# Identity matmuls ahead of the decay products, three more raw buffers, a later range check and an earlier copy of the ends in a GateLoop and ReLU-squared kernel

## The chip, the cores, the metric

One core of one Trainium2 chip. The metric is device time in microseconds (us) of one execution. "Kernel before" and "changed kernel" are the two sides.

## The reference

A gated linear recurrence with a complex decay per head channel, then a feed-forward block with squared ReLU:

```python
# q, k, v, a_re, a_im: (4, 8, 768, 48); w_in (384, 2048), w_out (2048, 384)
mag = np.sqrt(a_re * a_re + a_im * a_im)
scale = np.minimum(mag, 0.999) / (mag + 1e-06)
a_re_n, a_im_n = (a_re * scale, a_im * scale)
for t in range(S):
    new_re = ar * S_re - ai * S_im
    new_im = ar * S_im + ai * S_re
    S_re, S_im = (new_re + kv, new_im)          # kv = outer product of k[t], v[t]
    y[:, :, t] = np.einsum('bhd,bhde->bhe', q[:, :, t], S_re)
# ... y becomes x of (3072, 384)
h = x @ w_in
r = np.maximum(h, 0.0)
out = (r * r) @ w_out
```

## The kernel before

The work is cut into eight units of 384 tokens (n = 0 to 7). Each unit has a decay chain on VectorE (DVE) and ScalarE (ACT), four pairs of heads (h numbers the two heads of a pair) on TensorE (PE), and the dense products `h` (x by w_in) and `o` (g by w_out).

The kernel does not leave the order of instructions to the compiler. Every piece of work is a *step* with an engine, an assumed cost, a rank and a list of dependencies; a list scheduler written in the kernel walks them and fixes each engine's order:

```python
def step(key, engine, cost, rank, deps, fn, lag=None, bank=None, until=None):
    steps[key] = (engine, cost, ..., rank, deps, fn, bank, until)
# lay_out(): picks, per engine, the ready step that can start first; rank decides among near ties
for _, key in lay_out():
    emit(steps[key][5])          # fn() issues the instructions, in this order
```

`deps` decide only *where in its engine's order* a step is put. At run time an instruction waits for the data and buffers that it touches, and for nothing else.

The decay chain of a unit first sums logs inside groups of tokens (`in..`), copies the groups' ends to `last` (`e1`), transposes them on PE (`tot`), copies those to `e` on ACT, forms scan products on DVE (`product`, ten stages, writing `e`), and transposes back on PE (`bk`). After that PE adds the halves of complex products (`P`):

```python
one("iq", "ACT", act_cost(2 * NEL), lambda z: [(f"in{W - 1}3",)],      # squares
    lambda z: act.activation(out=whole(u["fa", z]), in_=whole(u["a", z]), func=AF.Square))
one("e1", "ACT", act_cost(2 * HH * D),                                 # copy of the ends
    lambda z: [(f"in{W - 1}3",), ("ap", n - 1, 0), ("ap", n - 1, 1)],
    lambda z: ends(z, 0))
...
product([NM, G - 1, 3], rest_of, rest_of, ...)                         # the last of ten stages
...
add(("bk", n, j), "PE", 330, deps, lambda j=j: transpose(...), rank=-3000, bank="tr", ...)
```

The weights arrive as 64-bit floats, 384 KB a piece, 16 pieces of w_in and 16 of w_out, and DVE and ACT convert them between the other work of units 0 and 1. A piece of w_out (i >= NF) is fetched into one of a few raw buffers once a conversion has freed it:

```python
else:
    deps = [("cv", i - (NF - NF // 2 if i < NF + NRAW else NRAW), 2)]
step(("fetch", i), "SP" if i >= NF else "POOL", ...)
```

In the last unit all 32 pieces are fetched again to check their range (`look`), into buffers of the chain, which is over by then:

```python
step(("look", i), "POOL", 800, 10 ** 6, [("inspect", i - 4), ("ap", n, 0), ("ap", n, 1)],
     lambda i=i: look(i), 5500)
```

Each pair of heads ends in `ypair` (PE), a copy to `yt` (ACT) and a transfer of its rows into `xT`, which `h` reads.

## Time and profile before

| | before |
|---|---|
| median of its runs | 766.58 us (4 runs, 765.14 to 768.22) |
| span of the profiled run | 765.2 us |
| PE busy | 702.8 us |
| PE waits of unit 0, up to 49 us | some 45 us |
| PE waits for unit 1's chain, 147 to 152 us | 5.08 us |
| PE wait in the last unit, before 605.81 us | 2.26 us |

The lines behind the table are shown in the prediction. PE is the bound nearly everywhere, so what counts is where it idles and where its clock is halved. The clock is read best from the distance of like instructions: a pair of `P` instructions starts every 0.49 us at full clock and every 0.96 us at half.

### The profile page before, as it was taken

To read this page: it belongs to the slowest core of one execution; us is meant where nothing else is said; L and a number is where in the kernel's file an instruction comes from. 1 tells how busy PE (TensorE), PEld (TensorE's weight loads), DVE (VectorE), ACT (ScalarE), POOL (GpSimd) and SP (SyncE) were. 2 spreads that over 40 slices of the span, in tenths; PEclk is the share of its full clock that TensorE was granted. 3 is DMA by queue.
4 is the path that set the end of the run, shared out by engine and by line. 5 is a ranking of instruction groups with operands and counts; after the bars stand their busy time and mean duration, and the time that the engine had idled before them with its cause. 6 is when DMAs were issued, how large, how long until landed. Compare 5 with 4: busy or idle time off the path is not lost.

```text
span 765.2 us, 9943 instructions
## 1 busy us (share of the span) xinstructions
PE 702.8 (92%) x3538; PEld 471.7 (62%) x3538; DVE 506.9 (66%) x1200; ACT 407.9 (53%) x754; POOL 114.3 (15%) x165
## 2 busy tenths in 40 slices
PE   0259999799999999999999999999999899999996
PEld 0138555477567766866776686568668555555553
DVE  4889988986688889579776966988992654000000
ACT  6646494346946676851877187746665103402500
POOL 5003100043004014010310121040011431000000
PEclk9999999989999999999999999999999999999999
DMA  9507760045007114220710252062023684000000
GB/s 271 182 18 227 236 220 12 22 145 145 1 1 255 38 50 159 84 57 21 249 47 17 92 178 53 0 204 82 27 74 112 212 292 136 3 18 14 0 11 24
DMA packets 39196, 76.25 MB, mean 100 GB/s; under 512 B 10881, under 2 KB 25313, under 8 KB 39137
## 3 DMA queue, kind: packets, MB, share of 16 engines
q0 software_dynamic: 14336, 53.88, 22.4%
q1 hardware_dynamic: 24672, 21.49, 9.2%
q8 instruction: 30, 0.49, 0.3%
q14 instruction: 30, 0.24, 0.1%
q10 hardware_dynamic: 128, 0.15, 0.1%
HBM read 56.62 MB, written 14.16 MB: 93 GB/s over the span
## 4 chain that ended last, share of the span: by engine, by line
PE 82%; DVE 10%; ACT 2%; DMA 2%; issue 1%; ACTq 0%; DVEq 0%; SPq 0%
PE h L1344 31%; PE o L1361 28%; PE sa L1238 6%; PE tq L1225 5%; PE kv L1252 3%; PE ypair L1274 3%; PE ypair L1279 2%; PE P L1111 2%; DMA xT<-yt 2%; DVE fa L991 2%; DVE e L998 1%; DVE fa L843 1%; PE bk L937 1%; PE tot L937 1%; DVE fb L816 1%
## 5 line engine op out<-in xcount | busy, mean ns | idle before, releaser
L1344 PE MATMUL h<-xT,w 128*128 128x384 f32 x768 | 255.5, 487 | 1.9 <-DMA xT<-yt 1.9
L1361 PE MATMUL o<-w,g 128*128 128x384 f32 x768 | 255.3, 488 | 0.0
L1361 PEld LDWEIGHTS o<-w,g 128*128 128x128 f32 x768 | 143.8, 191 | 94.5 <-issue 1.5
L1344 PEld LDWEIGHTS h<-xT,w 128*128 128x128 f32 x768 | 142.8, 190 | 95.0 <-issue 3.6
L1351 ACT ACTIVATE g<-h 128x384 f32<-128x384 f32 x128 | 62.2, 486 | 86.2 <-PE h L1344 86.0
L1230 ACT COPY QKT<-tq 96x512 f32<-96x512 f32 x96 | 76.6, 871 | 44.7 <-PE tq L1225 43.8
L1366 ACT COPY ot<-o 128x384 f32<-128x384 f32 x24 | 11.5, 477 | 124.4 <-PE o L1361 122.9
L1354 ACT ACTIVATE g<-g 128x384 f32<-128x384 f32 x128 | 66.1, 523 | 2.9
L1244 DVE TENSOR_TENSOR A<-sa,mask 128x384 f32<-128x384 f32 x64 | 35.3, 553 | 39.7 <-PE sa L1238 38.4
L991 DVE TENSOR_TENSOR fa<-e 128x192 f32<-128x192 f32 (+4 forms) x144 | 47.8, 371 | 18.4 <-ACT e L964 16.2
L1238 PE MATMUL sa<-QKT 96*128 96x128 f32 x384 | 54.7, 283 | 0.6 <-DVE QK L1117 0.6
L1238 PEld LDWEIGHTS sa<-QKT 96*128 96x128 f32 x384 | 48.1, 191 | 7.7 <-issue 2.4
L1225 PE MATMUL tq<-ident,QK 128*96 128x128 f32 x384 | 51.2, 273 | 0.9 <-ACT QKT L1230 0.9
L1225 PEld LDWEIGHTS tq<-ident,QK 128*96 128x96 f32 x384 | 42.6, 127 | 9.8 <-issue 5.6
L937 PE MATMUL tot<-ident,last 128*128 128x128 f32 x72 | 12.2, 295 | 31.4 <-ACT last L862 27.1
L1274 PE MATMUL ypair<-A,v 128*48 128x128 f32 x384 | 37.7, 281 | 3.3 <-ACT yt L1284 2.3
L808 DVE TENSOR_TENSOR fb<-fa 128x576 f32<-128x576 f32 x32 | 24.0, 753 | 22.2 <-ACT fa L904 12.2
L816 DVE SCALAR_TENSOR_TENSOR fb<-fb 128x576 f32<-128x576 f32 x48 | 35.0, 752 | 5.5 <-ACT fb L811 5.2
L1128 POOL DMA_DIRECT2D rows<-QK x20 | 12.7, 636 | 171.2 <-DVE QK L1117 171.2
L998 DVE TENSOR_TENSOR e<-fa,fa 128x96 f32<-128x96 f32 (+6 forms) x160 | 35.6, 284 | 2.6
L811 ACT ACTIVATE fa<-fb 128x576 f32<-128x576 f32 x48 | 31.2, 675 | 8.7 <-DVE fb L808 7.3
L1117 DVE TENSOR_TENSOR QK<-qk,fa 128x576 f32<-128x576 f32 x48 | 33.1, 751 | 0.0
(105 smaller groups left out, 828.8 us busy)
## 6 DMA issues: line engine op xcount, KB each, us to landing
rows<-QK POOLq DMA_DIRECT2D x12, 576.0 KB, 3.8
raw<-in_moe_w_in_dram POOLq DMA_DIRECT2D x16, 384.0 KB, 8.0
raw<-in_moe_w_out_dram SPq DMA_DIRECT2D x16, 384.0 KB, 4.0
look<-in_moe_w_in_dram POOLq DMA_DIRECT2D x16, 384.0 KB, 5.4
look<-in_moe_w_out_dram POOLq DMA_DIRECT2D x16, 384.0 KB, 4.3
out_dram<-ot SPq DMA_DIRECT2D x24, 192.0 KB, 1.9
v<-in_v_dram POOLq DMA_DIRECT2D x18, 192.0 KB, 4.2
a<-in_a_re_dram POOLq DMA_DIRECT2D x12, 288.0 KB, 3.5
```

Of the source, the lines that this page charges most:

```text
L816: dve.scalar_tensor_tensor(out=f[dst[-1]], in0=f[2] if i == 0 else f[dst[0]], scalar=scalar, in1=f[by], op0=ALU.add if i else ALU.mult, op ...
L991: dve.tensor_tensor(out=t, in0=x(e), in1=y(e)[:, j].unsqueeze(1) .to_broadcast(shape), op=ALU.mult)
L998: dve.tensor_tensor(out=dst(u["e"])[:, r], in0=temp(0)[:, r], in1=temp(1)[:, 1 - r], op=ALU.add if r else ALU.subtract)
L1225: nc.tensor.transpose(ps[:, 2 * j + h], src, ident)
L1230: act.copy(out=u["T", i].rearrange("r z (p c) -> r c z p", c=W)[:, c], in_=u["tq", i, c])
L1238: nc.tensor.matmul(sa[:, j], lhsT=T[:, 2 + h, ts(j, C)], rhs=T[:, h, ts(j, C)], start=True, stop=True)
L1244: dve.tensor_tensor(out=u["A", i][:, h], in0=u["sa", i, h], in1=mask3, op=ALU.mult)
L1274: nc.tensor.matmul(ypair[64 * h:64 * h + D, ts(j, C)], lhsT=u["v"][:, j, 2 * i + h], rhs=A[:, h, j], start=True, stop=S_j is None)
L1344: nc.tensor.matmul(u["h", f], lhsT=w1[:, f, m], rhs=u["xT"][:, m], start=(m == 0), stop=(m == NM - 1))
L1351: act.activation(out=t, in_=u["h", f], func=AF.Relu)
L1354: act.activation(out=u["g", f], in_=u["g", f], func=AF.Square)
L1361: nc.tensor.matmul(u["o", c], lhsT=u["g", f][:, ts(c, C)], rhs=w2[:, f], start=(f == 0), stop=(f == NF - 1))
```

## The change

Intent: keep PE's clock up by dummy matmuls before `bk` and `P` of units 0 and 1; feed the conversions of w_out from eight raw buffers instead of five; let the decay chain go on sooner by copying the ends before the squares; keep the range check's fetches from the last rows of xT. The core of the diff (cuts marked):

```diff
+    LENT = {NF + NRAW: "A", NF + NRAW + 1: "A", NF + NRAW + 2: "xT"}
 def fetch(i):
+        if i in LENT:                        # raw buffer borrowed from A tiles or an xT tile
+            ... = pool_.tile(shape, F32, name=tag, tag=tag)
 def weight_steps():
+            elif i in LENT:
+                deps = [("mix", 0, NP - 1), ("xT", 0, NP - 1, 1)]
+            elif i < NF + NRAW:
+                deps = [("cv", i - (NF - NF // 2), 2)]
             else:
-                deps = [("cv", i - (NF - NF // 2 if i < NF + NRAW else NRAW), 2)]
+                deps = [("cv", i - NRAW - (len(LENT) if i < NF + 2 * NRAW + len(LENT) else 0),
+                         2)]
 ...
             step(("look", i), "POOL", 800, 10 ** 6, [("inspect", i - 4), ("ap", n, 0),
-                 ("ap", n, 1)], lambda i=i: look(i), 5500)
+                 ("ap", n, 1)] + [("xT", n, NP - 1, h) for h in range(2)], lambda i=i: look(i),
+                 5500)
 ...
-        one("iq", ...)
-        one("e1", ...)
+        one("e1", ...)
+        one("iq", ...)
 ...
+        if n < 2:
+            def busy():
+                ps = dp.tile([C, L], F32, name="busy", tag="d")
+                for j in range(NM):
+                    nc.tensor.matmul(ps[:, ts(j, C)], lhsT=ident, rhs=ident, start=True,
+                                     stop=True)
+            for j in range(BUSY):            # BUSY = 9
+                add(("busy", n, j), "PE", 640,
+                    [("scan", n, 4, "plus", 1), ("busy", n, j - 1)], busy, rank=10 ** 6,
+                    bank="d", until=("busy", n, j))
 ... (the A step of unit 1's first pair and the xT steps of unit 2 get ("cv", f, 2) as deps)
```

More of the change, by code (lines that the diff above doesn't have):

```diff
@@ L653, in fetch @@
             return
-        raws[i] = (wst.tile([C, DM, 2], U32, name="raw", tag="raw")
-                   if i >= NF or NF // 2 <= i < FIRST else
-                   gp.tile([C, DM, 2], U32, name="raw", tag="g"))
+        if i in LENT:
+            pool_, tag, shape = {"A": (pr, "A", [C, 2, NM, C]),
+                                 "xT": (xp, "xT", [C, NM, L])}[LENT[i]]
+            t = pool_.tile(shape, F32, name=tag, tag=tag)
+            raws[i] = (t.rearrange("p a b c -> p (a b c)") if tag == "A" else
+                       t.rearrange("p a b -> p (a b)"))[:, 0:2 * DM].bitcast(U32).rearrange(
+                           "p (n two) -> p n two", two=2)
+        elif i >= NF or NF // 2 <= i < FIRST:
+            raws[i] = wst.tile([C, DM, 2], U32, name="raw", tag="raw")
+        else:
+            raws[i] = gp.tile([C, DM, 2], U32, name="raw", tag="g")
         queue.dma_start(
@@ L902, in chain_steps @@
             lambda z: measure(2 + z, parts(z)[3]))
+        one("e1", "ACT", act_cost(2 * HH * D),
+            lambda z: [(f"in{W - 1}3",), ("ap", n - 1, 0), ("ap", n - 1, 1)],
+            lambda z: ends(z, 0))
         one("iq", "ACT", act_cost(2 * NEL), lambda z: [(f"in{W - 1}3",)],
@@ L905, in chain_steps @@
                                      func=AF.Square))
-        one("e1", "ACT", act_cost(2 * HH * D),
-            lambda z: [(f"in{W - 1}3",), ("ap", n - 1, 0), ("ap", n - 1, 1)],
-            lambda z: ends(z, 0))
         one("ia", "DVE", D1, lambda z: [("iq",)], add_squares)
@@ L1319, in pair_steps @@
                  bank="sc", until=("A", n, i, h))
-            step(("A", n, i, h), "DVE", 480, -20, [("sa", n, i, h)],
+            step(("A", n, i, h), "DVE", 480, -20, [("sa", n, i, h)] + (
+                [("cv", f, 2) for f in LENT if LENT[f] == "A"] if x == NP else []),
                  lambda h=h: scored(h))
@@ L1333, in pair_steps @@
             step(("xT", n, i, h), "ACT" if aside(h) else "SP", 600 * len(list(pieces(h))), -24,
-                 [("y", n, i), ("h", n - 2, NF - 1)], lambda h=h: place(h), lag=2400)
+                 [("y", n, i), ("h", n - 2, NF - 1)]
+                 + [("cv", f, 2) for f in LENT if LENT[f] == "xT" and n == 2],
+                 lambda h=h: place(h), lag=2400)
     def dense_steps(u):
@@ L1433, in fast_path @@
     CONV = (500, 700)
+    BUSY = 9
     for b in range(B):
```

## The prediction

> **What bounds the kernel now.** I read the page first, then the waits of PE, then the timelines around each of its large waits, and last the windows of the stretch in which the second weights are converted.
>
> ```profile
> PE 702.8 (92%) x3538; PEld 471.7 (62%) x3538; DVE 506.9 (66%) x1200; ACT 407.9 (53%) x754; POOL 114.3 (15%) x165
> PE 82%; DVE 10%; ACT 2%; DMA 2%; issue 1%; ACTq 0%; DVEq 0%; SPq 0%
> ```
>
> PE is busy for 702.8 of 765.2 us. Only 62.4 us of idle time, and time lost to a half clock, can be won without touching the dense products. PE's waits say where the idle time is:
>
> ```profile
> PE tot L937 <- ACT last L862: 27.1, 1, 27.1
> PE bk L937 <- DVE e L998: 15.9, 2, 10.8
> PE tot L937 <- ACT last L864: 4.1, 2, 3.9
> PE ypair L1274 <- ACT yt L1284: 2.3, 1, 2.3
> ```
>
> Some 45 us lie ahead of 49 us, before the first unit's decay chain on DVE (scan of products, `e`) gives PE anything. The second wait of `bk` is 15.9 - 10.8 = 5.1 us at 147 to 152 us, where PE has used up unit 0's dense work and unit 1's chain is not done. The 2.3 us are in the last unit. Between 192 and 600 us PE has 407.06 of 408 us busy: nothing to win there. So I look at three places: unit 0 up to 86 us, unit 1 at 147 to 161 us, unit 7 at 603 to 612 us. PE has work queued behind each of them, so a microsecond won there is a microsecond of the end.
>
> The timeline of PE at unit 1 shows the clock besides the gap (start, duration, engine, instruction, count, idle time before it):
>
> ```profile
> 152.12 1.41 PE L937 MATMUL bk<-ident,e 128*128 128x128 f32 x6 [5.08 <-DVE e L998]
> 154.18 1.33 PE L1111 MATMUL P<-fa,ident 128*128 128x288 f32 x2 [0.65 <-DVE fa L1098]
> 155.30 1.17 PE L1111 MATMUL P<-fb,minus 128*128 128x288 f32 x2
> ...
> 160.94 0.65 PE L1111 MATMUL P<-fa,ident 128*128 128x288 f32 x2
> 161.43 0.65 PE L1111 MATMUL P<-fb,ident 128*128 128x288 f32 x2
> ```
>
> From start to start a pair of P instructions takes 0.96 us at first and 0.49 us from 159.1 us on: half clock, then full. Unit 0 looks the same: 0.96 us a pair from 49.19 us, 0.49 us from 53.2 us.
>
> The end of the kernel has the third place, first in the timeline of ACT, then in that of PE:
>
> ```profile
> 605.27 0.48 ACT L1284 COPY yt<-ypair 112x384 f32<-112x384 f32 x1 [5.81 <-DMA xT<-yt]
> 605.81 0.43 PE L1274 MATMUL ypair<-A,v 128*48 128x128 f32 x4 [2.26 <-ACT yt L1284]
> 606.28 0.64 PE L1274 MATMUL ypair<-A,v 128*48 128x128 f32 x4
> ```
>
> The xT rows that must leave a `yt` buffer were issued at 599.01 us and landed 6.19 us later in the chain of waits, while their median is 2.2 us. In that stretch POOL issues `look` fetches of the range check, 384 KB each. PE waits 2.26 us for it, and then goes on at half clock (four `ypair` take 0.43 us from start to start in place of 0.22).
>
> The windows around the conversion of the second weights (PE, PEld, DVE, ACT, POOL busy; clock, DMA share, GB/s):
>
> ```profile
> 86.00:100.00 14.00, 13.24 (x41) 7.90 (x42) 13.61 (x32) 11.11 (x24) 0.00 (x0) 1.00 0.96 324
> 100.00:113.00 13.00, 13.00 (x42) 7.64 (x41) 9.90 (x23) 12.06 (x26) 0.00 (x0) 1.00 0.66 207
> 113.00:124.00 11.00, 11.00 (x36) 6.50 (x35) 10.31 (x19) 5.57 (x13) 0.00 (x0) 1.00 0.14 43
> ```
>
> DVE is nearly full except for 3.1 us at 100 to 113 us and 0.7 us at 113 to 124 us. The unit 1 chain shares DVE with the conversions, and it is this chain that PE waits for at 147 us. DVE's own waits from 60 to 153 us:
>
> ```profile
> DVE w L683 <- ACT raw L665: 2.9, 3, 1.8
> DVE fa L991 <- ACT e L964: 2.0, 1, 2.0
> ```
>
> **What the Trainium skill says.** "TensorE: Matmul & The Clock Gate", What's actually happening: the array's clock is halved by default, and full only after a window of about 3.4 us of sustained work. The trace agrees: 0.96 against 0.49 us a pair, with the change 4.0 us (unit 0) and 4.9 us (unit 1) after the first P. The same page, Why this matters for your kernels, puts the idle gap that loses the clock at about 3 us; here 2.26 us were enough at 603.5 us, so I don't trust the threshold. "DMA: Bandwidth & Descriptors", Issuing engines are not separate DMA queues: transfers share the same 16 engines whoever issues them. The xT rows from SP that take 6.19 us beside POOL's `look` fetches agree. The same page, Specifications, gives a limit of about 358 GB/s per core from HBM; the trace has 324 GB/s at a DMA share of 0.96.
>
> **The change, part by part.** *Range check.* The 32 `look` fetches move behind all xT rows of the last unit. The rows should take their usual 2.2 us, be down by about 602 us, and PE's wait of 2.26 us goes. With it goes the half clock: the 24 `ypair` took 2.39 us (605.81 to 608.20) against 1.33 us for the same set in other pairs of this unit, 1.06 us, and the next 80 `o` took 26.75 us against 80 x 0.3225 = 25.8 us, 0.95 us. Sum **4.3 us**, all on the path. The checks themselves end at 642 us now; PE takes up their verdict at 663.9 us and the span ends at 765 us, so even 15 us later they cost nothing.
>
> *Identity matmuls.* Nine steps of three 128-column f32 matmuls in units 0 and 1, two instructions each as with P: 54 instructions. The P row gives 0.24 us for 288 columns at full clock, so 128 columns take 0.107 us, or 0.213 us at half clock. A set is 5.8 us at full clock, 11.5 us at half.
> - Unit 1: PE runs `o` until 147.04 us at full clock, and the set would reach to 152.8 us, past the 152.12 us at which `bk` starts. The clock stays up. It saves 0.66 us on `bk` (1.41 to 0.75) and ten P instructions at 0.24 us, 2.4 us. But DVE has only 0.50 + 1.10 + 0.22 = 1.8 us of waits for P in that stretch; freed from them it becomes the limit. I count **1.8 us**.
> - Unit 0: the set begins cold when the fifth product is done (41.0 us now). With a change of clock after 4 us, 19 instructions are cold and 35 at 0.107 us, 7.8 us in all, so it ends 2 us after `bk` could have started (46.66 us now, some 1.1 us earlier with the next part). Cold `bk` and P are then gone. DVE waits for P here for 0.54 + 1.10 = **1.6 us**, and this I count; the 1.1 us earlier start is lost to the late `bk`.
>
> *Order of the copy of the ends (`e1`) and the squares (`iq`).* With the copy first, `tot` and the copy to `e` come before or beside the squares. ACT needs 0.81 us for the two copies and 2.22 us for the squares; the 1.95 us for which DVE waits at 134.58 us shrinks by about **1.1 us**. This counts in unit 1; the later units are bound by PE.
>
> *Eight raw buffers.* Three more second-weight fetches can be in flight: two in A buffers, one in the other xT buffer, free in that stretch. No operation is added. Conversions no longer wait for a fetch that waits for a conversion. DVE has 3.1 + 0.7 us of idle time to win back between 100 and 124 us; with 324 GB/s already reached at 86 to 100 us the data can't come much sooner before 100 us, so I take two thirds, **2.4 us**. A first scores buffer of unit 1 now waits for two conversions that end some 50 us before, and unit 1's xT shares its buffer with unit 0's, whose last reader ended at 114 us: both free.
>
> In unit 1 the path gains 1.1 + 2.4 + 1.8 = 5.3 us. The upper limit is the gap and the cold work together, 5.08 + 0.65 + 3.1 = 8.8 us. Sum: 1.6 + 5.3 + 4.3 = 11.2 us, 765.26 - 11.2 = 754.1 us. Since the instruction order is laid out anew and such a layout seldom gives the whole sum, I put **755.0 us**.
>
> **Rivals.** *The identity matmuls get in the way.* PE works in order; steps laid behind `bk`, or ahead of it when the chain is earlier than the layout believes, are pure delay of 0.64 us each. For it: unit 0's set surely overruns by some 2 us, and if the chain of unit 1 comes 3.5 us earlier the 1.6 us of gap left can't hold a set of 5.8 us. Against it: they rank last, so `o` goes first, and nine fit the product stages left (41.0 to 46.7 us). If it happens, unit 1 gains about 2 and unit 0 nothing: some 759 us.
>
> *The transfers are hidden anyway.* Three more fetches may find the DMA engines full (0.96 share) and delay the last xT rows of unit 0, 4.57 us already, for which PE waits 1.2 us at 85.6 us. Then the buffers give 0 and this wait grows by about 1 us: some 758 us. For it speaks that 1.3 us of the conversions at 0.39 MB each needs nearly 300 GB/s.
>
> *More than I count.* If the chain of unit 1 comes early enough for the gap to vanish without the overrun, and the P stage is bound by PE instead of DVE, the whole 8.8 us come: some 750.5 us.
>
> **Range and chances.** The last unit's 4.3 us is the surest. Unit 0 gives 0 to 2.5, unit 1 gives 0 to 8.8. From 765.26 this is 749.7 at best and 761 with the last unit alone, and the extremes don't meet often: I take 750.0 to 760.5 us. Faster by over 2% needs less than 750.0 us, which nearly all parts at their best would give: 0.08. Slower by over 2% would need a new wait of 15 us: 0.01. Within 2%: 0.91.
>
> **What would show it.** In the last unit no wait of `ypair` for `yt`, xT rows landing in some 2.2 us, full clock there. In units 1 and 0 P pairs at 0.49 us from the first on, DVE without waits for P, `bk` in 0.75 us. In unit 0 `bk` behind the identity matmuls at about 48 us. At 100 to 124 us DVE idle for about 1.4 us instead of 3.8. The unit 1 squares behind the copy, and DVE's wait there below 1 us. I am wrong if P is cold still, if identity matmuls stand between `bk` and P, if `look` fetches still end late enough to hold up the verdict, or if a wait for the xT rows at 85 us has grown.

## The result

| | before | changed |
|---|---|---|
| runs | 4: 765.14 to 768.22 | 4: 758.75 to 760.16 |
| median | 766.58 us | 759.08 us |
| ratio of the means | | 0.9904 (0.9876 to 0.9932) |
| span of the profiled run | 765.2 us | 758.4 us |

All ratios here are the mean time of one kernel's fast runs over that of the other's of the same rounds, with a 95% interval, so not quite the ratio of the medians quoted. The change is within 2%, 7.5 us faster by the medians, 6.8 us by the profiled spans. The predicted 755.0 us (750.0 to 760.5) holds it, near the upper end. All outputs are right.

The profile's page of the changed kernel, busy times and chain that ended last:

```profile
PE 711.4 (94%) x3646; PEld 482.7 (64%) x3646; DVE 507.3 (67%) x1200; ACT 407.9 (54%) x754; POOL 114.3 (15%) x165
PE 79%; DVE 12%; DMA 4%; ACT 2%; issue 1%; POOL 0%; ACTq 0%
```

108 more PE instructions make PE 8.6 us busier, while the span shrinks by 6.8 us: "busy" here is partly filler. PE's waits (total us, times, longest):

```profile
PE bk L953 <- DVE e L1014: 4.2, 1, 4.2
...
PE kv L1281 <- DMA KC<-rows: 1.7, 3, 1.1
```

The 2.3 us of `ypair` for `yt` are gone, `bk` waits once instead of twice, and `kv` has waits for KC rows that the kernel before did not have. The timeline of PE in unit 0 (start, duration, engine, instruction, count, idle time before it):

```profile
34.88 7.47 PE L1058 MATMUL busy<-ident 128*128 128x128 f32 x54
46.50 1.54 PE L953 MATMUL bk<-ident,e 128*128 128x128 f32 x6 [4.15 <-DVE e L1014]
49.03 1.33 PE L1140 MATMUL P<-fa,ident 128*128 128x288 f32 x2 [0.99 <-DVE fa L1127]
```

The set ran at 34.88 us, as soon as PE had nothing else, and ended 4.15 us before `bk`, which took 1.54 us, and the first two `P` 1.33 us (0.75 when warm): cold as before. In unit 1:

```profile
146.97 3.51 PE L1058 MATMUL busy<-ident 128*128 128x128 f32 x30
150.32 0.82 PE L953 MATMUL bk<-ident,e 128*128 128x128 f32 x6
150.97 2.17 PE L1058 MATMUL busy<-ident 128*128 128x128 f32 x18
152.99 0.65 PE L1140 MATMUL P<-fa,ident 128*128 128x288 f32 x2
...
154.93 0.83 PE L1058 MATMUL busy<-ident 128*128 128x128 f32 x6
```

`bk` starts 1.80 us sooner (before: 152.12), warm, and so are all `P`. But 18 and 6 identity instructions stand behind `bk`. The windows of the conversions (columns as in the prediction):

```profile
86.00:100.00 14.00, 12.79 (x40) 7.47 (x40) 13.04 (x32) 10.33 (x23) 0.00 (x0) 1.00 1.05 361
100.00:113.00 13.00, 13.00 (x42) 7.65 (x41) 12.62 (x28) 11.31 (x23) 0.00 (x0) 1.00 0.58 215
```

DVE has 12.62 us of work in 100 to 113 us in place of 9.90. From 60 to 126 us SP's fetches waited 23.4 us for DVE's conversions to free a buffer, and wait 11.1 us now (22.2 us in no_lent below, which has five buffers again). By DVE's waits from 60 to 153 us, that for ACT's share of the conversions fell from 2.9 to 1.2 us, and that for the copy to `e` (2.0 us) is gone; but the squares now come second, and the wait for them grew from 1.3 to 2.1 us. In the last unit, PE, then the `look` fetches and the landing of the xT rows issued from 590 to 612 us:

```profile
595.60 5.32 PE L1393 MATMUL o<-w,g 128*128 128x384 f32 x16
600.92 0.43 PE L1303 MATMUL ypair<-A,v 128*48 128x128 f32 x4
```

```profile
L728 POOL DMA_DIRECT2D look<-in_moe_w_in_dram x12: 758/758/767, 582.0 to 597.5; - x12
```

```profile
DMA to landing us min/median/max: 3.5/4.2/4.9
```

The wait is gone, but not for the reason intended. The view begins at 575 us: four `look` fetches were issued from 561.0 us on already, and the next one starts at 582.0 us, 13.8 us ahead of the first of these xT rows (595.8 us). Nothing has been moved behind the rows.

To compare many kernels I cut each profiled run at three marks on PE: A, the first `h` of unit 0 that had waited for xT rows (86.76 us before), B, the same in unit 1 (190.96 us), and Y, the first `ypair` of the last pair (605.81 us). The table is worked out from the timelines (us).

| kernel | A | B − A | Y − B | of it, wait before Y | end − Y |
|---|---|---|---|---|---|
| before | 86.76 | 104.20 | 414.85 | 2.26 | 159.4 |
| changed, first profile | 87.53 | 100.03 | 413.36 | 0 | 157.5 |
| changed, second profile | 86.64 | 100.17 | 414.71 | 0.24 | 157.6 |
| no sets | 86.60 | 99.25 | 414.05 | 2.04 | 157.5 |
| no set in unit 0 | 86.22 | 100.56 | 416.96 | 0 | 157.7 |
| set held by data | 88.06 | 99.93 | 412.58 | 0 | 157.4 |
| no exchange | 87.27 | 100.54 | 415.36 | 2.09 | 159.1 |
| no extra buffers | 87.58 | 102.31 | 412.34 | 0.21 | 157.5 |
| before + `look` deps | 86.84 | 103.40 | 414.99 | 1.95 | 157.5 |
| before + held `look` | 87.24 | 104.27 | 413.03 | 0 | 157.5 |
| 15 steps, unit 0 | 85.20 | 100.03 | 412.59 | 0.48 | 157.5 |
| 5 steps, unit 1 | 86.94 | 99.42 | 412.79 | 0.60 | 157.7 |
| all three | 85.67 | 99.60 | 412.38 | 0 | 157.8 |

Between the first two rows: −0.8 (unit 0), +4.2 (unit 1), +1.5 (the middle: 2.26 of the wait less 0.8 elsewhere), +1.9 (behind Y, where the kernel before was at half clock for a while): 6.8 us. Warnings on the table: each row is one run. Between the two profiles of the changed kernel A differs by 0.9 us and Y − B by over 1 us. In the kernel before, "before + `look` deps" and "before + held `look`", PE has the same order of instructions up to 192 us, and still B − A reads 103.40 to 104.27 us. A difference of some 1 us in one column is no finding by itself.

### The profile page after: what moved, and what is told of

Read it like the earlier page.

```text
span 758.4 us, 10140 instructions
## 1 busy us (share of the span) xinstructions
PE 711.4 (94%) x3646; PEld 482.7 (64%) x3646; DVE 507.3 (67%) x1200; ACT 407.9 (54%) x754; POOL 114.3 (15%) x165
## 4 chain that ended last, share of the span: by engine, by line
PE 79%; DVE 12%; DMA 4%; ACT 2%; issue 1%; POOL 0%; ACTq 0%
PE o L1393 29%; PE h L1376 27%; PE sa L1267 5%; PE tq L1254 4%; PE kv L1281 3%; PE ypair L1303 3%; DMA KC<-rows 2%; PE ypair L1308 2%; DVE fa L1007 2%; PE P L1140 2%; DVE e L1014 2%; DMA xT<-yt 1%; DVE QK L1146 1%; DVE fa L1127 1%; DVE fb L1127 1%
```

## The experiments

Theory: each part has its own gain (unit 0 about nothing, unit 1 from the chain, the buffers and the clock, the last unit from the transfers). Rivals: `look` deps do nothing at all; the identity matmuls are not needed, or get in the way; the exchange carries more than unit 1. Each kernel was timed in five rounds against the kernel before. There were three jobs, on two chips; the kernel before had medians of 765.32, 766.04 and 765.47 us in them. Ratios are to the kernel before. after_again, busy1, gated and look_held were run in one job, with the changed kernel among them; the other medians are compared with the changed kernel across jobs. Where that matters, the ratios are the fairer measure: against 0.9906, the mean of the changed kernel's 0.9904 and 0.9908, and at 765.5 us, no_e1 is 4.8 us slower than the changed kernel, no_lent 4.1, no_busy 2.8 and u1_5 1.8 us, each uncertain by some 2 us (an estimate from the intervals).

### The first job: parts alone, or left out

**look_only**: the kernel before with one part.

```diff
 step(("look", i), "POOL", 800, 10 ** 6, [("inspect", i - 4), ("ap", n, 0),
-     ("ap", n, 1)], lambda i=i: look(i), 5500)
+     ("ap", n, 1)] + [("xT", n, NP - 1, h) for h in range(2)], lambda i=i: look(i), 5500)
```

> The kernel before with the range check's part of the change alone. Theory of the prediction: the 2.26 us wait of PE for yt in the last unit and the half clock after it go, 4.3 us faster than before (ratio about 0.994). Rival, from the traces of before and after: the added entries only move four look fetches behind one KC fetch in POOL's order and the verdict's matmul on PE; nothing makes POOL wait for the xT rows. Then the burst of looks still meets the rows, the 2.26 us wait stays, ratio 0.999 to 1.001.

Measured: 765.91 us, ratio 1.0013 (0.9994 to 1.0033). The wait of `ypair` stays:

```profile
PE ypair L1275 <- ACT yt L1285: 2.0, 1, 2.0
```

The `look` fetches begin at 575.8 us (572.2 us before), the xT rows at 598.2 us, and these take 5.1 us in the median to land. The dependency only moves four fetches behind another POOL transfer in POOL's order. The rows are issued by SP, POOL's fetch touches neither them nor `yt`, so POOL waits for nothing. The part by itself does nothing.

**e1_only**: the kernel before with the exchange of `e1` and `iq`.

```diff
-        one("iq", ...)
         one("e1", ...)
+        one("iq", ...)
```

> The kernel before with only the order of the ends' copy and the squares exchanged. Theory of the prediction: 1.1 us from unit 1 and nothing else (ratio 0.9985). Rival: exchanging two steps lays out all later units anew; the last unit's pairs then end some 14 us before the xT buffer is free, the looks start earlier than the xT rows instead of with them, and the 4.2 us of the last unit come from here; with 0.5 to 1 us of unit 1 the ratio is 0.993 to 0.994.

Measured: 763.57 us, ratio 0.9975 (0.9961 to 0.9989); by the medians 1.8 us faster. Its profiled run took 769.91 us, while the other six took 762.45 to 763.85, with cold `P` and 3.8 us of waits for KC rows; I take nothing about its parts from it.

**no_e1**: the changed kernel without that exchange.

```diff
-        one("e1", ...)
         one("iq", ...)
+        one("e1", ...)
```

> The changed kernel with the old order of the ends' copy and the squares. Theory of the prediction: 1.1 us slower than the changed kernel, the last unit's wait stays away (761 at a before of 766.6: ratio to before about 0.992). Rival: the last unit's 2.3 us wait and its half clock are back, and unit 1's gap of DVE: about 4 to 5 us slower than the changed kernel, ratio to before 0.996 to 0.997.

Measured: 763.41 us, ratio 0.9969 (0.9954 to 0.9984). It takes more than the predicted 1.1 us from the changed kernel: 4.3 us by the medians. In unit 1 only 0.4 to 0.5 us are missing (B − A), less than the scatter of that column. The rest is in the last unit: the wait before Y is back, and half clock behind it.

```profile
603.17 0.42 PE L1303 MATMUL ypair<-A,v 128*48 128x128 f32 x4 [2.09 <-ACT yt L1313]
...
604.36 0.65 PE L1308 MATMUL ypair<-QKT,St 96*48 96x128 f32 x4
```

Two steps exchanged on ACT change the order of every later unit, because all of it comes out of one scheduler. In the changed kernel the last `sa` of unit 7 starts at 579.38 us and 48 `h` follow it in one piece; in the kernel before it starts at 593.61 us with 12 `h` behind it. The `look` fetches stand differently to the xT rows too. POOL's timeline of the kernel before, whose xT rows were issued from 598.5 us on, and of the changed kernel, rows from 595.8 us on:

```profile
596.27 1.61 POOL L713 DMA_DIRECT2D look<-in_moe_w_in_dram  x2 [19.99 <-DVE look L722]
598.09 1.62 POOL L713 DMA_DIRECT2D look<-in_moe_w_in_dram  x2 [0.21 <-DVE look L722]
```

```profile
582.03 1.61 POOL L728 DMA_DIRECT2D look<-in_moe_w_in_dram  x2 [18.00 <-DVE look L737]
583.85 1.62 POOL L728 DMA_DIRECT2D look<-in_moe_w_in_dram  x2 [0.21 <-DVE look L737]
...
596.57 0.76 POOL L728 DMA_DIRECT2D look<-in_moe_w_in_dram  x1 [2.04 <-DVE odd L739]
597.54 0.76 POOL L728 DMA_DIRECT2D look<-in_moe_w_in_dram  x1 [0.21 <-DMA look<-in_moe_w_in_dram]
```

In both, four fetches are issued in a burst after 18 to 20 us of none. Before, the burst falls around the start of the rows; in the changed kernel it comes 13.8 us ahead of them, and at the start of the rows the fetches come one by one. That fits the 4.2 us of landing against 4.8, but it is a reading of two traces, not a test, and no_busy below speaks against it.

**no_busy**: the changed kernel without identity matmuls.

```diff
-    BUSY = 9
+    BUSY = 0
```

> The changed kernel without the identity matmuls. Theory of the prediction: 3.4 us slower than the changed kernel (1.8 in unit 1, 1.6 in unit 0). From the trace of after: in unit 0 the set ran at 34.9 to 42.3 us, went cold again and cost about 0.8 us, so leaving it out wins 0.8 there; in unit 1 the cold P costs 2 to 3 us while the 24 late identity matmuls no longer delay P by 1 us: about 1 us slower than the changed kernel, ratio to before 0.991 to 0.993.

Measured: 759.95 us, ratio 0.9943 (0.992 to 0.9966): 0.9 us slower than the changed kernel by the medians, and one run of 764.75 us among its six. Its profile (757.4 us) is shorter than the changed kernel's:

```profile
148.72 0.97 PE L953 MATMUL bk<-ident,e 128*128 128x128 f32 x6 [2.51 <-DVE e L1014]
150.78 0.75 PE L1140 MATMUL P<-fa,ident 128*128 128x288 f32 x2 [1.09 <-DVE fa L1127]
```

PE idles 2.51 us before `bk`, and yet keeps the clock: `P` is warm from the first on. B − A is 99.25 us against 100.03 and 100.17 with the sets. That is within the scatter of the column, so the traces show no gain of unit 1's set, and no cost: with the gap down from 5.08 to 2.51 us by the other parts, there was no cold work left to save in this run. The times do not quite agree: by the ratios the sets together are worth some 2.8 us, 0.8 us of it from the one run of 764.75 us. The kernel also has the exchange, and its burst of `look` fetches (from 579.0 us) is as far ahead of its first xT row (592.8 us) as in the changed kernel, 13.8 us; and still PE waits 2.04 us before Y, with xT rows landing in 5.1 us. So neither the exchange nor early `look` fetches are enough to end that wait. That it hangs on where the order laid out happens to put both is my reading, not shown.

### The second job: the changed kernel again, and two doubted mechanisms

**after_again**: the changed kernel, no edit.

> The changed kernel once more, as the yardstick of the others on this chip. Ratio to before 0.990 to 0.993. The first profile of it had the last unit's yt ready 0.05 us before PE needed it; if that was luck of the transfers, this profile may show a wait of ypair of up to 2 us.

Measured: 759.12 us (758.08 to 760.80), ratio 0.9908 (0.9885 to 0.9932). The result repeats. The wait before Y is 0.24 us here; in the first profile `yt` was ready 0.05 us before PE needed it. And this profile lost clock where the first did not:

```profile
367.49 2.21 PE L1281 MATMUL kv<-v,KC 128*96 128x48 f32 x24 [1.14 <-DMA KC<-rows]
369.54 3.86 PE L1376 MATMUL h<-xT,w 128*128 128x384 f32 x6
```

In the first profile the same wait was 1.15 us and the same six `h` took 2.17 us. This is a lottery of 1.7 us inside one kernel.

**busy1**: the changed kernel without unit 0's set.

```diff
-        if n < 2:
+        if n == 1:
```

> The changed kernel without unit 0's 27 identity matmuls; the order of instructions is otherwise the same. Theory of the prediction (they keep P warm, 1.6 us): 1.6 us slower than the changed kernel. Rival, from the trace after: nothing in the data holds them behind the fifth product, they run at 34.9 to 42.3 us, the clock is lost again before bk at 46.5 us, and P is cold in either case: no difference within 0.5 us, or slightly faster, as the set may shift the point at which the clock rises (54.5 us in the changed kernel, 53.2 us in the kernel before).

Measured: 761.0 us, ratio 0.9934 (0.991 to 0.9959), 1.9 us slower than the changed kernel by the medians. The trace does not show why. A is 86.22 us, against 87.53 and 86.64 with the set, so unit 0 is no slower without it. What its profiled run lost lies between B and Y, where a wait of 1.28 us for KC rows at 495.22 us was followed by half clock. But that run was the slowest of the six. What unit 0's set gains, if anything, stays open.

**gated**: the changed kernel with one matmul ahead of unit 0's set that reads what the fifth product writes, so that the set really starts there, as I had assumed.

```diff
+                if first:
+                    nc.tensor.matmul(ps[:, 0:1], lhsT=ident, rhs=u["e"][:, 0, 0, 15:16],
+                                     start=True, stop=True)
```

> The changed kernel with one more matmul ahead of unit 0's identity matmuls, which reads a column that the fifth product wrote, so that the set begins at about 40.6 us in truth, as the prediction assumed. Prediction's working: set cold for some 4 us, done at about 48 us, bk right behind it warm, P pairs at 0.49 us from the first on, 1.6 us faster in unit 0 than without; against the changed kernel 1.6 to 2.4 us faster. Rival: bk late by some 2 us eats what the warm P wins, difference below 0.5 us.

Measured: 759.75 us, ratio 0.9924 (0.99 to 0.9948); not told apart from the changed kernel.

```profile
41.22 9.11 PE L1061 MATMUL busy<-ident 128*128 128x128 f32 x54
50.16 0.82 PE L953 MATMUL bk<-ident,e 128*128 128x128 f32 x6
51.72 0.75 PE L1145 MATMUL P<-fa,ident 128*128 128x288 f32 x2 [0.73 <-DVE fa L1132]
```

The set begins at 41.22 us, and `bk` and `P` are warm as I had hoped. But `bk` starts 3.7 us later (46.50 to 50.16), and A is 88.06 us, later than in any other kernel. Even with the assumption made true the predicted gain of unit 0 is not there.

**look_held**: look_only with a copy on POOL that reads xT, ahead of the fetches in POOL's order; now they must wait.

```diff
+        landed = const.tile([C, NM], F32, name="landed")
+        step(("landed",), "POOL", 100, 10 ** 6, [("xT", n, NP - 1, h) for h in range(2)],
+             lambda: pool.tensor_copy(out=landed, in_=u["xT"][:, :, 0]))
-                 ("ap", n, 1)] + [("xT", n, NP - 1, h) for h in range(2)], ...
+                 ("ap", n, 1), ("landed",)], ...
```

> The kernel before, with POOL made to wait in truth: a copy of three columns of the last unit's xT stands ahead of the range check's fetches, and reads all its rows. Theory of the prediction: xT rows land in 2 to 3 us, PE's wait of 2.0 to 2.3 us for yt goes, and the half clock where it follows: 2.3 to 4.3 us faster than before (ratio 0.994 to 0.997). Rival: ten rows' transfers from one queue, or the fetch of instructions, are slow by themselves, the wait stays above 1 us: ratio 0.999 to 1.001. The verdict comes some 12 us later and delays nothing.

Measured: 764.17 us, ratio 0.9971 (0.9947 to 0.9996): 1.9 us by the medians, 2.2 by the ratio. PE's first `ypair` of the last pair, with no idle time before it, and the landing of the xT rows:

```profile
604.54 0.43 PE L1278 MATMUL ypair<-A,v 128*48 128x128 f32 x4
```

```profile
DMA to landing us min/median/max: 1.8/2.0/2.3
```

Without `look` fetches beside them (the first starts at 610.3 us) the rows land in 2.0 us in place of 4.8, and the wait is gone. So the transfers' competition was read rightly, and ending it is worth about the size of the wait; the change just does not end it.

### The third job: buffers, lengths of the sets, and a combination

**no_lent**: the changed kernel with five raw buffers.

```diff
-    LENT = {NF + NRAW: "A", NF + NRAW + 1: "A", NF + NRAW + 2: "xT"}
+    LENT = {}
```

> The changed kernel with five raw buffers as before. Theory of the prediction: DVE gets its idle time of some 3.5 us between 95 and 125 us back, the chain of unit 1 is 2.4 us later, and the identity matmuls ahead of bk fill a gap that is longer again; about 2.4 us slower than the changed kernel (ratio to before about 0.994 where the changed kernel has 0.991). Rival: DVE is nearly full in either case and the fetches are bound by the transfers, so unit 1's bk moves by less than 1 us and the time by less than 1 us.

Measured: 762.2 us, ratio 0.996 (0.9939 to 0.9981): 3.1 us slower than the changed kernel by the medians. The window of the conversions, and PE at unit 1:

```profile
100.00:113.00 13.00, 13.00 (x42) 7.70 (x41) 11.40 (x25) 12.75 (x27) 0.00 (x0) 1.00 0.66 197
```

```profile
152.77 0.91 PE L953 MATMUL bk<-ident,e 128*128 128x128 f32 x6
```

DVE is back to 11.40 us, `bk` comes 2.45 us later than at 150.32, and B − A is 2.1 to 2.3 us longer. This is the surest part of the change.

**u0_15**: 15 steps in unit 0, laid out from the first product on, so that the set reaches up to `bk`.

```diff
-            for j in range(BUSY):
+            for j in range((15, 9)[n]):
-                    [("scan", n, 4, "plus", 1), ("busy", n, j - 1)], busy, rank=10 ** 6,
+                    [("scan", n, (0, 4)[n], "plus", 1), ("busy", n, j - 1)], busy, rank=10 ** 6,
```

> The changed kernel with 15 identity steps in unit 0 instead of 9, laid out from the first product on. They run without a data dependency from 34.9 us, 54 instructions in 7.5 to 8 us and 36 more at 0.107 us, so the set should end at 46.2 to 46.7 us, just at bk. Theory that a clock kept up until bk makes P warm: bk in 0.75 us, P pairs at 0.49 us from 49 us on, 1 to 2 us faster than the changed kernel. Rival: an overrun past 46.5 us, or DVE as the limit of the P stage, leaves less than 0.5 us.

Measured: 757.9 us, ratio 0.9904 (0.9884 to 0.9925).

```profile
35.02 11.45 PE L1058 MATMUL busy<-ident 128*128 128x128 f32 x90
46.65 0.97 PE L953 MATMUL bk<-ident,e 128*128 128x128 f32 x6 [0.18 <-DVE e L1014]
49.18 0.75 PE L1140 MATMUL P<-fa,ident 128*128 128x288 f32 x2 [1.56 <-DVE fa L1127]
```

`bk` and `P` are warm, `bk` not late, and A is 85.20 us, 1.4 to 2.3 us earlier than in the changed kernel and 1.0 to 1.4 us earlier than in the two kernels that differ from it by having no set in unit 0. all_three below, with the same set, has 85.67 us, 0.5 to 0.9 us earlier than those two. `P` now waits for DVE. So the idea of the set in unit 0 is right, if it ends at `bk`, for a gain near the scatter of A. The times agree in direction only: 1.2 us by the medians across jobs, nothing by the ratios.

**u1_5**: 5 steps instead of 9 in unit 1, so that none stands behind `bk`.

```diff
-            for j in range(BUSY):
+            for j in range((9, 5)[n]):
```

> The changed kernel with five identity steps in unit 1 instead of nine: the four that stand between bk and P and among P go. P should begin right behind its fa (about 0.9 us earlier) and not be interrupted (0.66 us): up to 1.5 us faster. Rival: the gap of 1 to 1.5 us between bk and P then costs the clock, or DVE is the limit of the P stage and the identity matmuls there cost nothing: no difference within 0.7 us.

Measured: 759.74 us, ratio 0.993 (0.9907 to 0.9953); not told apart from the changed kernel (one run of 763.12 us is among its six). In the trace `P` starts at 151.28 us in place of 152.99, but 0.6 us of this were won before A. B − A is 99.42 us, 0.6 to 0.8 us less, which is within its scatter. `P` waits for DVE twice here (0.73 and 0.47 us), as the rival held.

**all_three**: 15 steps in unit 0, 5 in unit 1, and the held `look` fetches (edits as above).

> The changed kernel with 15 identity steps in unit 0, five in unit 1, and the range check's fetches held in truth behind the last rows of xT. If each wins what its own theory says (1 to 2, 1.5, and 0 to 2 us in the last unit), 755 to 757 us and a ratio to before of 0.985 to 0.989; if the rivals hold, equal to the changed kernel within 1 us (0.990 to 0.992).

Measured: 757.15 us (756.72 to 758.04), ratio 0.9891 (0.9869 to 0.9912). No `ypair` wait, xT rows in 2.0 us. It has the lowest median of all, about 2 us below the changed kernel by the medians and 1.0 to 1.3 us by the ratios, without a round in common. Against the kernel before it is 1.1%, so still within 2%.

## Why the prediction was right, and where it was not

The total fell into the range, 4 us above the point. Its sum was 11.2 us, and the profiles give 6.8. Step by step:

- **What bounds the kernel** held: what was won lies in unit 1 and in the last unit, two of the three places named, and between 192 and 600 us nothing was to be won.
- **Unit 0, 1.6 us predicted, −0.8 measured** (+0.1 in the second profile). The step that failed reads "the set begins cold when the fifth product is done". I took the scheduler's dependency for a wait. The matmuls read only `ident`, so PE ran them at 34.88 us and was idle again for 4.15 us before `bk`. The step would have failed anyway: gated makes it true, and there the set took 9.11 us, not 7.8, and the overrun, predicted as 2 us, was 3.7 us and ate the gain. u0_15 and all_three show what was right in it: warm `P` gives 0.5 to 1.4 us in the traces, against no set at all, if the set meets `bk`.
- **Unit 1, 5.3 us predicted, 4.2 measured.** The buffers were put at 2.4; leaving them out lengthens B − A by 2.1 to 2.3, so this term was right, by DVE's idle time and the fetches that no longer wait for a conversion, as argued. The exchange was put at 1.1; leaving it out costs 0.4 to 0.5 here, not clear of the scatter. The copy to `e` does come earlier, but DVE then waits longer for the squares (2.1 us in place of 1.3). The identity matmuls were put at 1.8; the set itself gave nothing in the traces, as no_busy is not slower in this stretch (0.8 to 0.9 us quicker). `P` was warm there by the shorter gap alone. The remainder of the 4.2 us, some 1.5, I put down to this warm `P`: it is argued from the sum, no run isolates it.
- **The last unit, 4.3 us predicted, 4.2 measured, by another mechanism.** That the sizes match is luck. The step that failed reads "The 32 `look` fetches move behind all xT rows": look_only does nothing, and the trace of the changed kernel has the fetches alongside. Nor is the sum right where the step is made true: look_held won 1.9 to 2.2 us, about the wait of 2.26 us, and not 4.3. The other 2 us, half clock behind Y, were read from one trace and need not follow such a wait: look_only ran on at full clock (157.5 us behind Y) after a wait of 1.95 us. The changed kernel's gain here came with the new order that the exchange led to, since no_e1 loses it; why is open, since no_busy has the exchange and the wait too.
- **The exchange as a whole** was the worst-sized term: 1.1 us predicted, 4.3 by leaving it out and 1.8 by itself. Both hold for this kernel, and I would expect neither to carry over, since most of it is a shift of unit 7's order.
- **Rival one**, identity matmuls in the way, was right in kind: 24 of unit 1's 54 instructions stand behind `bk`, and gated has the overrun. It cost under 1 us, since DVE was the limit there.
- **Rival two**, transfers hidden or delayed: the DMA share did rise to 1.05 with 361 GB/s at 86 to 100 us, but the wait for xT rows at 87 us did not grow (1.21 against 1.18 us). What I had not foreseen were new waits for KC rows (1.15 us at 368.27 us and 0.35 us at 495.68 us in the first profile), another result of the new order: the −0.8 between B and Y.
- **Rival three**, more than I count, did not happen: no term came out above its value but the exchange.

Open: what unit 0's nine steps gain (busy1's times against its trace), whether the sets together gain nothing (traces) or up to some 3 us (times of no_busy), and what exactly makes xT rows take 4.2 us in one order and 5.1 in another with `look` fetches beside them in both.

## What to carry to other kernels

Before counting on a "dependency", ask which instruction reads or writes what: in a kernel that lays out its own order, a dependency without shared data is a place in a queue, not a wait, and a filler matmul without an input runs as soon as the engine is free. A filler must end where the real work begins: too early, and the clock falls again; too late, and it delays; shortening the gap itself may make it needless. When one scheduler orders everything, test each part both alone and left out, since a small exchange can gain most in a stage that it does not touch.

## What the Trainium skill lacked or had wrong

- "TensorE: Matmul & The Clock Gate", Why this matters for your kernels and What you observe: an idle gap of about 3 us that loses the clock did not decide here. A wait of 1.14 us was followed by half clock (six `h` in 3.86 us), one of 1.15 us in another profile of the same kernel was not (2.17 us); 2.26 us lost it in the kernel before, 2.51 us in no_busy did not. So even a wait of one microsecond is a lottery of 1.7 us. And the return to full clock, which the page puts at about 4 us of sustained work, give or take 0.5 us, varied more here: 54 identity instructions took 7.47, 7.98 and 9.11 us in unit 0. At 0.112 us warm (30 of them in the 3.35 us ahead of unit 1's `bk`) and 0.213 us cold (estimated from the `P` row) some 13, 18 and 29 of them were cold, which is 2.7, 3.8 and 6.1 us from the set's start (estimates). The prediction took 4.0 and 4.9 us, counted from the first `P`, as agreement with the page's 3.4 us window; these lie within that spread and agree only roughly. The end of a filler is uncertain by as much.
- The same page, Seeing it yourself, warns that the trace's clock events can't be fully trusted, and this is borne out. It names a check by a throttle counter; a simpler one is missing: the granted clock of the windows reads 1.00 for the kernel before from 49.2 to 53.2 us, where `P` pairs start every 0.96 us, the spacing of half clock. The spacing is the safer reading.
- "DMA: Bandwidth & Descriptors", Specifications, agreed: its limit of about 358 GB/s from HBM was about met, with 361 GB/s of all transfers, most of them loads from HBM, at a share of 1.05. What it lacks is what sharing does to a small transfer: xT rows of 24 to 72 KB landed in 2.0 us alone (look_held, median) and in 4.8 us (up to 6.2) beside fetches of 384 KB (before).
